# K and V loaded by even and odd partitions in a decode attention kernel

## The chip, the cores and the metric

The kernel runs on one core of one Trainium2 chip. The metric is device time in microseconds, measured on the chip; a lower time is better.

## The reference

Two branches share an input `x` of four tokens (batch 4, one query position, width 512) and are mixed by a gate of each token. The first is attention over the last 4096 positions of a long cache, with 32 query heads on 8 key heads; the second is a gated feed-forward layer. Cut to what matters:

```python
g = sigmoid((x * gate_w).sum(-1, keepdims=True))
# attention: B=4, Hq=32, Hkv=8, Dh=128, Sk=16384, window W=4096
q = (x @ wq).reshape(B, 1, Hq, Dh).transpose(0, 2, 1, 3)
k = repeat(k_cache[:, :, Sk - W:, :], 4, axis=1)
v = repeat(v_cache[:, :, Sk - W:, :], 4, axis=1)
p = softmax(einsum("bhqd,bhkd->bhqk", q, k) * Dh ** -0.5)
a = einsum("bhqk,bhkd->bhqd", p, v).transpose(0, 2, 1, 3).reshape(B, 1, Hq * Dh) @ wo
# feed-forward, F=1792
gate = x @ W_gate; up = x @ W_up
b = ((gate * (gate > 0)) * up) @ W_down
out = g * a + (1 - g) * b
```

All inputs are bfloat16. The window of K and of V is 32 MB each; with the weights 81 MB are read.

## The kernel before

The attention is worked in eight sets. A set is half of a batch entry: four of its eight key heads, 4096 keys each, so 4 MB of K and 4 MB of V. `Ksb` holds two sets of K (set `s` in half `s % 2`), `Vsb` one set of V; before that `Vsb` holds `wq`.

**Layout of a set.** The 4096 keys of a head are cut into 32 rows of 128 keys. Partition 4r + h of `Ksb` and `Vsb` holds row r of head h (`heads`, L245): 128 keys of 128 elements, 32 KB without a break. One transfer brings a set of K, and one a set of V.

**A set's work.** `turned` (L366) transposes K in blocks of 32 x 32 words on VectorE (DVE), in two halves of 4096 words a partition; a word is two bfloat16 elements. Its output `KT` has the elements on the partitions, and on the free side 2048 words a head: the word of head h, row r lands at 2048h + 8n + r%8, so that the 32 words of one block (4 heads, 8 rows) go to 32 places, the heads 2048 words apart. `scores` (L371) multiplies these by the queries `qS` into the PSUM tile `SB`. `highest` (L382) takes the maximum of each query head, with a small product on PE to turn it, and leaves `negmax`. `powers` (L392) forms the exponentials on ScalarE (ACT) and spreads them by four products into `PB`. `evicted` (L400) copies `PB` to `pP` in two halves on ACT, in the order of K's partitions, and adds them up. `turned_p` (L407) transposes `pP` on DVE, `values` (L414) multiplies with V on PE ("PV"), `summed` (L424) adds the parts, and `select` and `normal` (L434, L438) divide by the sum.

**Order of the work.** Each engine runs its own list of instructions in the order in which the program writes them. In a set DVE does the maximum, then the first half of the next set's K transpose, `normal` of the set before, the two transposes of P, the second half of the next K transpose, and `summed`. PE runs the eight sets as a loop (`emit`, L132); the other engines but SyncE run their lists inside `once` (L114), a loop body that is run one time. SyncE (SP) runs its list straight.

**Order of the loads.** All large loads are issued by SP, in this order: `wq`, K0, K1, V0, K2, V1, ... K7, V6, gate and up weights, V7, down weights, and `wo` in six parts into the place of `KT`. SP waits before an issue: K of set s for the K transpose of set s - 2 (`KTC`), V of set s for PV of set s - 1, `wo` for the last scores. A wait that names an instruction counted on a semaphore which PE reads is turned into a wait for the next instruction of that engine on the engine's own semaphore (`need`). The semaphore `V` is shared by `wq` and all V loads; PE lowers it by one set's count in each turn. At the end SP waits for both halves of the output row on `fin` and stores it.

Of the kernel before, what the change touches and what calls it, by code (L numbers as in the profile page):

```python
# [7 lines left out]
ACTF = mybir.ActivationFunctionType  # L8
# [4 lines left out]
SK = 16384  # L13
WIN = 4096
# [14 lines left out]
class Program:  # L29
# [101 lines left out]

    def emit(self, nc, engine, eng, sems):  # L132
        ops = self.ops[engine]
        if engine == "sp":
            self.emit_list(eng, sems, engine, ops, {}, {})
            return
        with self.once(nc, engine, eng):
            if engine != "pe":
                self.emit_list(eng, sems, engine, ops, {}, {})
                return  # L140
            t = self.turns
            self.emit_list(eng, sems, engine, ops[:t[0]], {}, {})
            first = self.signature(t[0], t[1], {})
            for k in range(1, len(t) - 1):
                shift = {s: k * n for s, n in self.lowered.items() if s not in self.shared}
                assert self.signature(t[k], t[k + 1], shift) == first, k
            turn = eng.alloc_register("pe_set")
            eng.reg_mov(turn, 0)
            eng.br("pe_loop")
            with nc.body("pe_loop", valid_engines=bass.OrderedEngineSet([eng.engine])):  # L150
                self.emit_list(eng, sems, engine, ops[t[0]:t[1]], {}, {}, turn)
                eng.drain()  # L152
                for s, n in self.lowered.items():
                    eng.sem_inc(sems[s], -n)
                eng.reg_add(turn, turn, 1)
                eng.br_lt(turn, len(t) - 1, on_true="pe_loop", on_false="pe_loop_end")
            nc.switch_bb("pe_loop_end")
            shift = {s: (len(t) - 1) * n for s, n in self.lowered.items() if s not in self.shared}
            self.emit_list(eng, sems, engine, ops[t[-1]:], shift, {})


def bass_gated_mix__sliding_block_cached__glu_gated_reglu__decode_kernel(
# [13 lines left out]
    with ExitStack() as ctx:  # L176
        def sb(name, shape, dt):
            return ctx.enter_context(nc.sbuf_tensor(name, shape, dt))

        def ps(name, width):  # L180
            return ctx.enter_context(nc.psum_tensor(name, [128, width], FP32))

        Ksb = sb("Ksb", [128, 2, 16384], BF16)
        Vsb = sb("Vsb", [128, 16384], BF16)
        KT = sb("KT", [128, 8192], FP32)
# [26 lines left out]
        p = sb("p", [128, 512], BF16)  # L212
        pP = sb("pP", [128, 2048], BF16)
# [9 lines left out]
        outr = sb("outr", [4, 512], BF16)  # L223
        SB = ps("SB", 512)
        PB = ps("PB", 2048)
# [3 lines left out]

        Kw = Ksb[:, :, :].rearrange("p s w -> p (s w)").bitcast(FP32).rearrange("p (s w) -> p s w", s=2)  # L230
        Kt = KT[:, :].bitcast(BF16).rearrange("p (h c v r o) -> p h c v r o", h=4, v=2, r=8, o=2)
        Kn = KT[:, :].rearrange("p (h n r) -> p n r h", h=4, r=8)
        qall = Wff[:, 0:4096]
        qrow = Wff[:, 4096:5120]
        hrelu = Kw[:, 0, 0:FQ]
# [6 lines left out]
        P = Program()  # L242
        P.events[("V", -1)] = ("V", 16, None, 0)

        def heads(cache, s):  # L245
            b, half = s // 2, s % 2
            return cache[b, 4 * half:4 * half + 4, SK - WIN:SK, :].rearrange("h (r c) d -> r h (c d)", r=32)

        def load_k(s):
            P.dma("sp", lambda e: e.dma_start(Ksb[:, s % 2, :], heads(A_k_cache, s)), ("K", s),  # L250
                  [("KTC", s - 2, 1)] if s >= 2 else [])

        def load_v(s):
            P.dma("sp", lambda e: e.dma_start(Vsb[:, :], heads(A_v_cache, s)), ("V", s),
                  [("PV", s - 1) if s else ("Q",)], sem="V")
            P.events[("V", s)] = ("V", 32, None, 0)

        P.op("dve", lambda e: e.memset(xs[:, :], 0.0), ("XS0",))
        for b in range(4):
            P.dma("act", lambda e, b=b: e.dma_start(xs[b:128:32, :], A_x[b].rearrange("o (a c) -> (o a) c", a=4)),  # L260
                  ("X", b), [("XS0",)])
        P.dma("act", lambda e: e.dma_start(xs[4:128:32, :], gate_w.rearrange("(a c) -> a c", a=4)), ("X", 4), [("XS0",)])
        load_k(0)
        for s in range(1, NSET):
            load_k(s)
            load_v(s - 1)
        P.dma("sp", lambda e: e.dma_start(Wff[:, 0:4 * FF], B_W_gate.rearrange("(p t) f -> p (t f)", p=128)), ("WG",), [("QT", 1)])
        P.dma("sp", lambda e: e.dma_start(Wff[:, 4 * FF:8 * FF], B_W_up.rearrange("(p t) f -> p (t f)", p=128)), ("WU",), [("QT", 1)])
        load_v(NSET - 1)
        P.dma("sp", lambda e: e.dma_start(Wd[:, :, :].rearrange("p i w -> p (i w)"),  # L270
                                          B_W_down.rearrange("(p i) w -> p (i w)", p=128)), ("WD",))
        wo_src = A_wo.rearrange("(p i) w -> p i w", p=128)
        for k in range(len(WO_CUTS) - 1):
            lo, hi = WO_CUTS[k], WO_CUTS[k + 1]
# [90 lines left out]

        def turned(s, u):  # L366
            lo = 4096 * u
            P.op("dve", lambda e: e.transpose(Kn[:, 128 * u:128 * u + 128], Kw[:, s % 2, lo:lo + 4096]), ("KTC", s, u),  # L368
                 [("K", s), ("SC", s - 1, u) if s else None], sem="vd")

        def scores(s):  # L371
# [28 lines left out]
        def evicted(s):  # L400
            for k in range(2):
                P.op("act", lambda e, k=k: e.activation(  # L402
                    pP[:, 1024 * k:1024 * k + 1024].rearrange("p (c r h) -> p c r h", r=8, h=4),
                    PB[:, :].rearrange("p (h c r) -> p c r h", h=4, r=8)[:, 32 * k:32 * k + 32], ACTF.Copy,
                    accum_out=rows[:, 2 * (s % 2) + k:2 * (s % 2) + k + 1]), ("PTE", s, k), [("PERM", s), ("RS", s - 2) if s > 1 else None])

        def turned_p(s):  # L407
# [49 lines left out]
        def units():  # L457
# [11 lines left out]
                ("H",), [("H2",), ("G",), ("HT0",)], sem="vd")  # L469

        turned(0, 0)
        turned_q(0)
        P.op("dve", lambda e: e.memset(osum[:, 0:64], 0.0), ("PTT", -1, 0), sem="vd")
        P.op("dve", lambda e: e.memset(mrow[:, 0:1], 0.0), ("PTT", -1, 1), sem="vd")
        turned(0, 1)
        turned_q(1)
        P.op("dve", lambda e: e.memset(osum[:, 64:129], 0.0), ("OSB", -1), sem="vd")
        for s in range(NSET):
            load_q(s)
            P.turn_edge()  # L480
            scores(s)
            highest(s)
            powers(s)
            evicted(s)
            select(s - 1)
            if s < NSET - 1:
                turned(s + 1, 0)
            else:
                P.op("dve", lambda e: e.memset(zz[:, :], 0.0), ("KTC", NSET, 0), sem="vd")
            if s:  # L490
                normal(s - 1)
            turned_p(s)
            P.op("pe", "aside")
            if s == NSET - 1:
                at = len(P.ops["pe"])
                gateup()
                P.aside = (at, len(P.ops["pe"]))
                units()
            else:
                turned(s + 1, 1)  # L500
            values(s)
            summed(s)
# [31 lines left out]
        for u in range(2):  # L534
# [3 lines left out]
        P.op("act", lambda e: e.copy(outr[:, 256:512], AB[32:36, 256:512]), ("FIN", 1), [("ACC", 1)], sem="fin")  # L538

        P.op("pool", None, None, [("ACC", 1)])  # L540

        per = {sem: P.events[b][1] - P.events[a][1] for sem, a, b in (
            ("vd", ("MX", 1), ("MX", 2)), ("va", ("EXP", 1), ("EXP", 2)), ("pq", ("QS", 1, 3), ("QS", 2, 3)))}
        per["V"] = 16
        P.shared["V"] = True
        P.lowered = per

        names = list(P.ENGINES) + ["vd", "va", "pq", "pro", "fin"] + P.dmas + ["done"]
        sems = {name: ctx.enter_context(nc.semaphore(name)) for name in names}
        nc.sync.dma_start(Vsb[:, :], A_wq.rearrange("(p t) w -> p (t w)", p=128)).then_inc(sems["V"], 16)  # L550
        with nc.Block() as block:
            @block.sync
            def _(e):
                P.emit(nc, "sp", e, sems)
                e.wait_ge(sems["fin"], 2)
                e.dma_start(out.rearrange("b o d -> (b o) d"), outr[:, :]).then_inc(sems["done"], 16)

            @block.gpsimd
            def _(e):
                P.emit(nc, "pool", e, sems)  # L560

            @block.tensor
            def _(e):
                P.emit(nc, "pe", e, sems)

            @block.vector
            def _(e):
                P.emit(nc, "dve", e, sems)

            @block.scalar  # L570
            def _(e):
                P.emit(nc, "act", e, sems)
# [29 lines left out]
```

## Time and profile before

| | us |
|---|---|
| median of three runs | 214.65 (213.74 to 215.91) |
| profiled execution | 215.62 |
| its span, first to last instruction | 214.1 |
| DVE busy | 167.4 (78%) |
| PE busy | 101.4 (47%) |
| ACT busy | 30.9 (14%) |

The transfers read 81.01 MB at a mean of 378 GB/s, and the mean granted clock of TensorE (PE) was 0.85. The span is the time between the first and the last instruction; the profiled execution's own time is a little longer than it. A share of busy time is a mean over the lead-in, the eight sets and the tail, which have different limits.

In the rows of the profile, L368 is line 368 of the kernel; "out<-in" names the tiles; "x16" is the number of instructions in a group, and the figures behind the bar are busy time in us, the mean duration in ns, and the idle time of the engine just before the group with what ended it. In the chain of waits a row is the start, the length and the work. SPq is SP's queue of issues.

### The profile page before, as it was taken

How to read it: one execution, taken by the hardware profiler on the slowest of the kernel's cores; microseconds unless marked ns; L12 is line 12 of the kernel's file. 1: busy time of each engine (PE TensorE's matmuls, PEld its weight loads, DVE VectorE, ACT ScalarE, POOL GpSimd, SP SyncE). 2: the span in 40 equal slices, each digit the busy share in tenths (PEclk: the TensorE clock that was granted, in tenths of full speed). 3: DMA queues.
4: the chain of work that ended last, by engine and by line, in shares of the span. 5: the costliest groups of instructions: out<-in, count | busy, mean ns of one | idle time of the engine just before them, and what ended most of it. 6: DMA issues, size and time to landing. Idle time of an engine off the chain costs nothing.

```text
span 214.1 us, 1792 instructions
## 1 busy us (share of the span) xinstructions
PE 101.4 (47%) x693; PEld 45.0 (21%) x701; DVE 167.4 (78%) x121; ACT 30.9 (14%) x49; POOL 15.4 (7%) x54
## 2 busy tenths in 40 slices
PE   0007433535650763085309430843195329477895
PEld 0002001112320331032104210320042013234362
DVE  0001799699989998999899989999998999745500
ACT  1100550040013003100400050005000500150000
POOL 7006110100010001000100100010001000000000
PEclk9999999999998599759966975796559656966999
DMA  7999999996399999998999799999977998898980
GB/s 288 398 454 429 398 484 392 380 410 288 98 404 478 392 386 398 453 429 318 465 410 465 300 465 416 392 386 398 441 343 294 392 433 351 331 453 384 415 328 4
DMA packets 4050, 81.03 MB, mean 378 GB/s; under 512 B 460, under 2 KB 976, under 8 KB 1232
## 3 DMA queue, kind: packets, MB, share of 16 engines
q1 hardware_dynamic: 4008, 81.01, 90.2%
q14 instruction: 2, 0.02, 0.0%
q10 hardware_dynamic: 40, 0.01, 0.0%
HBM read 81.01 MB, written 0.00 MB: 378 GB/s over the span
## 4 chain that ended last, share of the span: by engine, by line
DVE 65%; DMA 16%; PE 10%; issue 5%; PEldq 2%; PEld 1%; SPq 0%
DVE KT L368 47%; DMA Ksb<-in_A_k_cache_dram 10%; DVE pT L409 7%; DMA Vsb<-in_A_v_cache_dram 6%; PE AB L506 4%; DVE osum L431 3%; PE OB L419 3%; DVE mx L384 2%; PE FO L386 2%; PEldq L152 2%; DVE osb L425 1%; DVE on L442 1%; DVE oT L444 1%; DVE mrow L388 1%; PE SB L376 1%
## 5 line engine op out<-in xcount | busy, mean ns | idle before, releaser
L368 DVE STREAM_TRANSPOSE KT<-Ksb 128x4096 f32<-128x4096 f32 x16 | 116.5, 7282 | 4.8 <-DMA Ksb<-in_A_k_cache_dram 4.8
L419 PE MATMUL OB<-Vsb,pT 128*64 128x512 bf16 x256 | 44.8, 527 | 48.7 <-DVE pT L409 46.6
L419 PEld LDWEIGHTS OB<-Vsb,pT 128*64 128x64 bf16 x256 | 19.5, 150 | 73.2 <-DVE pT L409 51.7
L376 PE MATMUL SB<-KT,qS 128*32 128x512 bf16 x256 | 19.4, 428 | 19.9 <-DVE KT L368 8.4
L394 ACT ACTIVATE p<-SB,negmax 128x512 bf16<-128x512 f32 x8 | 5.5, 687 | 125.9 <-DVE negmax L388 125.9
L409 DVE STREAM_TRANSPOSE pT<-pP 128x1024 bf16<-128x1024 bf16 x16 | 18.8, 1211 | 0.2
L402 ACT ACTIVATE pP<-PB 128x1024 bf16<-128x1024 f32 x16 | 16.2, 1019 | 11.4 <-PE PB L397 11.4
L362 POOL COPY qS<-qT 32x64 bf16<-32x64 bf16 x32 | 7.3, 229 | 135.7 <-PE SB L376 125.3
L376 PEld LDWEIGHTS SB<-KT,qS 128*32 128x32 bf16 x256 | 9.2, 146 | 30.2 <-DVE KT L368 12.0
L397 PE MATMUL PB<-p,perm 128*128 128x512 bf16 x24 | 8.5, 476 | 11.1 <-ACT p L394 11.1
L315 DVE STREAM_TRANSPOSE xz<-xs 128x128 bf16<-128x128 bf16 x1 | 0.3, 312 | 15.7 <-DMA xs<-in_gate_w_dram 15.7
L322 PE MATMUL FO<-zr,onesf 128*128 128x4 f32 x2 | 0.6, 364 | 17.7 <-DVE zr L320 17.7
L431 DVE TENSOR_REDUCE osum<-osb 128x128 f32<-128x512 f32 x8 | 8.6, 1070 | 0.3
L425 DVE TENSOR_TENSOR osb<-OB,emask 128x512 f32<-128x512 f32 x8 | 5.4, 672 | 3.9 <-PE OB L419 3.9
L386 PE MATMUL FO<-identw,mx 128*128 128x128 f32 x16 | 4.2, 348 | 8.6 <-DVE mx L384 8.6
L506 PE MATMUL AB<-KT,oq 128*36 128x512 bf16 x30 | 6.6, 379 | 0.0
L537 DVE CAST outr<-AB 4x256 bf16<-4x256 f32 x1 | 0.4, 411 | 7.6 <-PE AB L509 7.6
L388 DVE CUSTOM_DVE_ANT_0 mrow<-FO,qmask 128x128 f32<-128x128 f32 x8 | 2.3, 292 | 4.9 <-PE FO L386 4.9
L384 DVE TENSOR_REDUCE mx<-SB 128x1 f32<-128x512 f32 x8 | 5.4, 679 | 0.9 <-PE SB L376 0.9
L397 PEld LDWEIGHTS PB<-p,perm 128*128 128x128 bf16 x32 | 2.8, 107 | 13.1 <-ACT p L394 10.5
L386 PEld LDWEIGHTS FO<-identw,mx 128*128 128x128 f32 x16 | 2.6, 202 | 12.8 <-DVE mx L384 12.8
L342 PE MATMUL PB<-Wff,rall 128*128 128x512 bf16 x8 | 3.8, 626 | 3.1 <-ACT Wff L346 2.0
(66 smaller groups left out, 64.8 us busy)
## 6 DMA issues: line engine op xcount, KB each, us to landing
Ksb<-in_A_k_cache_dram SPq DMA_DIRECT2D x8, 4096.0 KB, 18.7
Vsb<-in_A_v_cache_dram SPq DMA_DIRECT2D x8, 4096.0 KB, 12.4
Vsb<-in_A_wq_dram SPq DMA_DIRECT2D x1, 4096.0 KB, 12.3
Wff<-in_B_W_gate_dram SPq DMA_DIRECT2D x1, 1792.0 KB, 16.2
Wff<-in_B_W_up_dram SPq DMA_DIRECT2D x1, 1792.0 KB, 19.8
Wd<-in_B_W_down_dram SPq DMA_DIRECT2D x1, 1792.0 KB, 16.1
KT<-in_A_wo_dram SPq DMA_DIRECT2D x1, 1536.0 KB, 17.3
KT<-in_A_wo_dram SPq DMA_DIRECT2D x1, 1024.0 KB, 19.4
```

The costliest lines, as they stand in the source:

```text
L362: P.op("pool", lambda e, src=src, dst=dst: e.tensor_copy(dst, src[:, :, :, b, :]), ("QS", s, a), [("QT", half), ("QS", s, a - 1) if a else ...
L368: P.op("dve", lambda e: e.transpose(Kn[:, 128 * u:128 * u + 128], Kw[:, s % 2, lo:lo + 4096]), ("KTC", s, u), [("K", s), ("SC", s - 1, u) ...
L376: P.op("pe", lambda e, u=u, vo=vo, h=h: e.matmul(SB[32 * h:32 * h + 32, :], qS[:, 16 - 16 * u:48 - 16 * u, 4 * h + vo], Kt[:, h, 64 * u:64 ...
L384: P.op("dve", lambda e: e.tensor_reduce(mx[:, :], SB[:, :], AXIS.X, ALU.max), ("MX", s), [("SC", s, 1)], sem="vd")
L386: P.op("pe", lambda e: e.matmul(FO[:, 128:256], mx[:, 0:1].to_broadcast([128, 128]), identw[:, :], start=True, stop=True), ("MT", s), [("M ...
L397: P.op("pe", lambda e, h=h: e.matmul(PB[:, 512 * h:512 * h + 512], perm[:, h, :], p[:, :], start=True, stop=True), ("PERM", s) if h == 3 e ...
L402: P.op("act", lambda e, k=k: e.activation(pP[:, 1024 * k:1024 * k + 1024].rearrange("p (c r h) -> p c r h", r=8, h=4), PB[:, :].rearrange( ...
L409: P.op("dve", lambda e, k=k: e.transpose(pT[:, :].rearrange("p (u c q) -> p c u q", u=2, c=64)[:, 32 * k:32 * k + 32], pP[:, 1024 * k:1024 ...
L419: P.op("pe", lambda e, g=g, blk=blk, n=n: e.matmul(OB[64 * g:64 * g + 64, :], pT[:, 64 * blk:64 * blk + 64], Vsb[:, 512 * blk:512 * blk + ...
L425: P.op("dve", lambda e: e.tensor_tensor(osb[:, :, :], OB[:, :].rearrange("p (e d) -> p e d", e=4), emask[:, :].rearrange("p (e o) -> p e o ...
L431: P.op("dve", lambda e: e.tensor_reduce(osum[:, 0:128], osb[:, :, :].rearrange("p e d -> p d e"), AXIS.X, ALU.add), ("OSB", s), [("OM", s) ...
L506: P.op("pe", lambda e: e.matmul(AB[0:36, :], stat, mov, start=start, stop=False), None, waits)
```

## The change

K and V of a set are loaded by two transfers each, one to the even and one to the odd partitions. Partition 8a + 2h + b now holds row 2a + b of head h, so that two neighbouring rows of a head lie side by side. K's transpose then writes the 32 words of a block as 16 runs of two neighbouring words; `KT` itself holds the same words in the same places as before, and the products on it are the same. `evicted` puts P into the new order of partitions and reads `PB` in runs of two. The two transfers of a K share one semaphore, and those of a V count twice on theirs. K's load waits for `NEGMAX` of set s - 2 instead of its K transpose. SP's list runs inside `once` like those of the other engines, and the store of the output becomes the last entry of that list.

```diff
     def emit(self, nc, engine, eng, sems):
         ops = self.ops[engine]
-        if engine == "sp":
-            self.emit_list(eng, sems, engine, ops, {}, {})
-            return
         with self.once(nc, engine, eng):
...
-        Kn = KT[:, :].rearrange("p (h n r) -> p n r h", h=4, r=8)
+        Kn = KT[:, :].rearrange("p (h n b) -> p n h b", h=4, b=2)
...
-        def heads(cache, s):
+        def rows_of(cache, s, w):
             b, half = s // 2, s % 2
-            return cache[b, 4 * half:4 * half + 4, SK - WIN:SK, :].rearrange("h (r c) d -> r h (c d)", r=32)
+            return cache[b, 4 * half:4 * half + 4, SK - WIN:SK, :].rearrange("h (a b c) d -> b a h (c d)", a=16, b=2)[w]
 
         def load_k(s):
-            P.dma("sp", lambda e: e.dma_start(Ksb[:, s % 2, :], heads(A_k_cache, s)), ("K", s),
-                  [("KTC", s - 2, 1)] if s >= 2 else [])
+            for w in range(2):
+                P.dma("sp", lambda e, w=w: e.dma_start(Ksb[w:128:2, s % 2, :], rows_of(A_k_cache, s, w)), ("K", s, w),
+                      [("NEGMAX", s - 2)] if s >= 2 else [], sem="K%d" % s)
+            P.events[("K", s)] = ("K%d" % s, 32, None, 0)
 
         def load_v(s):
-            P.dma("sp", lambda e: e.dma_start(Vsb[:, :], heads(A_v_cache, s)), ("V", s),
-                  [("PV", s - 1) if s else ("Q",)], sem="V")
-            P.events[("V", s)] = ("V", 32, None, 0)
+            for w in range(2):
+                P.dma("sp", lambda e, w=w: e.dma_start(Vsb[w:128:2, :], rows_of(A_v_cache, s, w)), ("V", s, w),
+                      [("PV", s - 1) if s else ("Q",)], sem="V")
+            P.events[("V", s)] = ("V", 48, None, 0)
...
         def turned(s, u):
             lo = 4096 * u
-            P.op("dve", lambda e: e.transpose(Kn[:, 128 * u:128 * u + 128], Kw[:, s % 2, lo:lo + 4096]), ("KTC", s, u),
+            P.op("dve", lambda e: e.transpose(Kn[:, 512 * u:512 * u + 512], Kw[:, s % 2, lo:lo + 4096]), ("KTC", s, u),
...
                 P.op("act", lambda e, k=k: e.activation(
-                    pP[:, 1024 * k:1024 * k + 1024].rearrange("p (c r h) -> p c r h", r=8, h=4),
-                    PB[:, :].rearrange("p (h c r) -> p c r h", h=4, r=8)[:, 32 * k:32 * k + 32], ACTF.Copy,
+                    pP[:, 1024 * k:1024 * k + 1024].rearrange("p (n h b) -> p n h b", h=4, b=2),
+                    PB[:, :].rearrange("p (h n b) -> p n h b", h=4, b=2)[:, 128 * k:128 * k + 128], ACTF.Copy,
...
+        P.dma("sp", lambda e: e.dma_start(out.rearrange("b o d -> (b o) d"), outr[:, :]), ("OUT",), [("FIN", 1)], sem="done")
...
-        per["V"] = 16
+        per["V"] = 32
...
                 P.emit(nc, "sp", e, sems)
-                e.wait_ge(sems["fin"], 2)
-                e.dma_start(out.rearrange("b o d -> (b o) d"), outr[:, :]).then_inc(sems["done"], 16)
```

More of the change, by code (lines that the diff above doesn't have):

```diff
@@ L540, in bass_gated_mix__sliding_block_cached__glu_gated_reglu__decode_kernel @@
         P.op("pool", None, None, [("ACC", 1)])
+        P.dma("sp", lambda e: e.dma_start(out.rearrange("b o d -> (b o) d"), outr[:, :]), ("OUT",), [("FIN", 1)], sem="done")
         per = {sem: P.events[b][1] - P.events[a][1] for sem, a, b in (
             ("vd", ("MX", 1), ("MX", 2)), ("va", ("EXP", 1), ("EXP", 2)), ("pq", ("QS", 1, 3), ("QS", 2, 3)))}
-        per["V"] = 16
+        per["V"] = 32
         P.shared["V"] = True
         P.lowered = per
-        names = list(P.ENGINES) + ["vd", "va", "pq", "pro", "fin"] + P.dmas + ["done"]
+        names = list(P.ENGINES) + ["vd", "va", "pq", "pro", "fin"] + P.dmas
         sems = {name: ctx.enter_context(nc.semaphore(name)) for name in names}
```

## The prediction, made before the changed kernel was run

> **What bounds the kernel now.** I read the page first, for the share of each engine and of the transfers, then the chain of waits, then the transfers in stretches, then single rows.
>
> ```profile
> span 214.1 us, 1792 instructions
> DVE  0001799699989998999899989999998999745500
> DMA  7999999996399999998999799999977998898980
> q1 hardware_dynamic: 4008, 81.01, 90.2%
> ```
>
> Two resources stand close together. VectorE (DVE) is nearly solid from the fifth slice to the thirty-fifth, and the 16 DMA engines are busy for 90.2% of the span with 81.01 MB. Which of them sets the pace shows in the chain, here one of the eight sets (a set is half a batch: four heads):
>
> ```profile
> 121.58 1.07 DVE osum L431
> ...
> 124.13 0.01 DVE negmax L388
> 124.14 7.12 DVE KT L368
> 131.26 0.04 DVE rc L441
> ...
> 132.17 2.37 DVE pT L409 x2
> 134.55 7.33 DVE KT L368
> 141.87 0.52 DVE osb L425
> ...
> 142.48 1.08 DVE osum L431
> 143.56 0.61 DVE mx L384
> ```
>
> From one L431 to the next it is 142.48 - 121.58 = 20.9 us, DVE row after DVE row, with waits only for the small products around the maximum. Two transposes of K make 14.5 us of it on the chain (2 x 7.28 = 14.6 by instruction), and everything else 6.3 us. So the middle is bound by DVE.
>
> The transfers follow it closely:
>
> ```profile
> 5.00:40.00 35.00, 1.00 1.00 431
> 41.00:44.00 3.00, 1.00 0.83 284
> 53.80:57.40 3.60, 1.00 0.00 0
> 57.40:160.60 103.20, 0.79 0.97 406
> 160.60:162.20 1.60, 1.00 0.00 0
> ```
> ```profile
> Ksb<-in_A_k_cache_dram SPq DMA_DIRECT2D x8, 4096.0 KB, 18.7
> Vsb<-in_A_wq_dram SPq DMA_DIRECT2D x1, 4096.0 KB, 12.3
> Wff<-in_B_W_gate_dram SPq DMA_DIRECT2D x1, 1792.0 KB, 16.2
> ```
>
> The stretch columns are window, length, granted TensorE clock, DMA share, GB/s. With a full queue the rate is 431 GB/s, so 4096 KB (4.194 MB) take 9.73 us and 1792 KB 4.26 us. One set needs K and V, 19.46 us of transfer, against 20.9 us of DVE. The transfers have only 1.4 us of slack in a set: whatever DVE gains beyond that is not seen in the period.
>
> **The change part by part.**
>
> *K's transpose, L368.* Same words in, same count; the words of a 32-word run now go out as 16 pairs of neighbours instead of 32 words that each lie 2048 words from the one before.
>
> ```profile
> L368 DVE STREAM_TRANSPOSE KT<-Ksb 128x4096 f32<-128x4096 f32 x16 | 116.5, 7282 | 4.8 <-DMA Ksb<-in_A_k_cache_dram 4.8
> L444 DVE STREAM_TRANSPOSE oT<-on 32x128 f32<-32x128 f32 x8 | 3.2, 395 | 0.3
> L351 DVE STREAM_TRANSPOSE qT<-Wff 128x1024 f32<-128x1024 f32 x2 | 2.4, 1200 | 0.0
> L464 DVE STREAM_TRANSPOSE Ksb<-Ksb 128x448 f32<-128x448 f32 x1 | 0.6, 645 | 0.0
> ```
>
> L351 and L464 write neighbouring words: (1200 - 645)/(1024 - 448) = 0.96 ns a word and 213 ns fixed. L444 writes words four apart and comes to (395 - 213)/128 = 1.42 ns; L368 to (7282 - 213)/4096 = 1.73 ns. So a scattered word costs up to 0.76 ns extra. No row writes pairs. Lower end: a pair hides the extra, 213 + 4096 x 0.96 = 4.2 us (4.8 if L351 is simply scaled by four). Middle: the extra is paid once per pair, 5.7 us. Upper end: nothing changes, 7.3 us. A pair is nearer to L351 than to single words; I take 4.9 us. The choice matters little: DVE's set becomes 2 x 4.9 + 6.3 = 16.1 us, and DVE falls below the transfers' 19.46 us for any price under 6.6 us.
>
> [...]
>
> *The loop through PE.* With DVE out of the way the loop is: PV products, scores of the next set, its maximum, K's transpose, `normal`, P's transpose, PV again.
>
> ```profile
> 133.47 5.02 PE L419 MATMUL OB<-Vsb,pT 128*64 128x512 bf16 x32 [7.13 <-DVE pT L409]
> 154.38 6.50 PE L419 MATMUL OB<-Vsb,pT 128*64 128x512 bf16 x32 [6.82 <-DVE pT L409]
> 162.04 2.06 PE L376 MATMUL SB<-KT,qS 128*32 128x512 bf16 x32 [1.16 <-PEq L154]
> ```
>
> PV 5.0 to 6.5 us, the loop's turn and both halves of the scores 1.16 + 2.06 = 3.2, maximum to K's next transpose 1.5 (in the chain 121.58 + 1.07 = 122.65 to 124.14), transpose 4.9, `normal` 0.9 (131.26 to 132.17), first half of P's transpose 1.2: 16.8 to 18.3 us. That too is under 19.46, by at least 1.2 us.
>
> *The wait of K's load.* It moves from the K transpose two sets back (which SP sees at the next counted DVE instruction, L428) to `NEGMAX`.
>
> ```profile
> 80.02 0.07 DVE osum L428
> ...
> 82.64 0.01 DVE negmax L388
> ```
> ```profile
> 56.10 0.54 SPq L254 DMA_DIRECT2D Vsb<-in_A_v_cache_dram  x1
> ...
> 80.05 0.54 SPq L250 DMA_DIRECT2D Ksb<-in_A_k_cache_dram  x1
> ```
>
> That is 2.6 us later. Behind it on SP waits only the next V, whose own release (PV done) comes some 14 us later, so V is not held. In the new order K's issue falls about 10.5 us after a V has landed (PV 5.5, scores 3.2, maximum 1.5), while the next V keeps the queue full until about 19.5 us: cost nothing. V's issue is the tighter one: PV ends up to 6.5 us after V has landed, landing trails the last bytes by about half a microsecond, and first bytes follow an issue by 57.4 - 56.10 = 1.3 us. Together 8.3 us, under the 9.73 us of the K load in flight: 1.4 us to spare.
>
> *Two loads for one.* 16 more issues on SP at 0.54 us, four instead of two in a set; SP otherwise waits, and the second half is issued while the first flows. Same bytes, same 32 KB rows, same set of 128 partitions in the end. What a load on every other partition yields, no row shows. Bounds: the full 431 GB/s, 9.73 us for two halves, or half of it, 19.46 us, as if only half of the memory's inputs could be used at once; a gain is excluded since the queue was full at 431. The nearest row is the whole load with the same rows and bytes; I take 9.73.
>
> *The rest.* ACT's L402 reads pairs from PSUM instead of single words; even twice its 1 us a half would end before P's transpose, which stands behind K's on DVE. SP inside `once` adds a few register instructions, hidden by `A_wq` in flight for 12.3 us. The output's issue and its waits keep their place.
>
> *The sum*, if the queue stays full from the start until the last V:
>
> ```profile
> 1.27 21.47 DMA Ksb<-in_A_k_cache_dram
> ...
> 181.58 12.40 DMA Vsb<-in_A_v_cache_dram
> ...
> 211.51 0.39 DVE outr L537
> ```
>
> K of set 0 lands at 22.74. Then come 15 loads of 9.73 (7 K, 8 V) = 146.0 and two of 4.26 = 8.5 (gate and up, ahead of the last V): the last V lands at 177.2 instead of 193.98. From there to the span's end it was 214.1 - 193.98 = 20.1 us, PV, down and output products, whose own loads follow V in the queue as before: 197.3. The 16.7 us come from the empty stretches (3.6 + 1.6), the slow one at 284 GB/s, and 406 GB/s instead of 431 over 103 us. The profiled execution took 215.62, 1.5 more than its span, and lay 1.0 above the median of 214.65; so 197.3 + 1.5 - 1.0 = **198 us**.
>
> Own range 195 to 204: down if the tail tightens, up by a slow stretch of 3 us and a price of 5.7 us with PV at 6.5.
>
> **The rivals.**
>
> *Slower: the half loads don't reach the rate.* The source of a half load has 16 slices of 2 rows x 128 keys (`a`), four heads each. If each of 16 DMA engines takes one slice, then it writes partitions 8a, 8a+2, 8a+4, 8a+6, and all engines in step sit at the same place in their eights: half of the neighbourhoods of four partitions are written by two engines each, half by none. For it: no load in the trace is of this kind. Against it: the same 32 KB rows run at 431 now, and engines out of step would not meet. Price: 13.0 (K of set 0 lands at 22.74, 9.73 before that `A_wq`) + 16 L + 8.5 + 20.1 + 0.5, with L the time of one K or V (9.73 gives the 198 again). It decides from L = 10.8 us on (389 GB/s), where the result is 214.65. Two cases: engines that meet half of the time, L = 14.6, **276 us**, with anything from 214 to 300; and always, 19.46, 353 us.
>
> [...]
>
> *Gaps in the queue.* The 1.4 us before V's issue is lost to a slow PE clock, and each of seven sets pays up to 1.3 us of first-byte latency: 203 to 211 us, say 207. For it: PV already took 6.5 us; against it: 5.0 to 5.5 is usual.
>
> *The transposes stay at 7.3 us,* the change not doing what it says: DVE's 20.9 us a set stays, K's later issue is covered, 215 us. L444 speaks against it.
>
> **How the numbers follow.** Forecast 0.41; half loads that meet in part 0.27, always 0.19; gaps 0.08; unchanged transposes 0.05. The half loads together weigh a little more than the forecast, since nothing in the trace bears on them either way, but over 140 us; 198 is the likeliest case. A measurement of this kernel (213.74 to 215.91) can tell about 1% from no change. Faster by over 1%: 0.41 + 0.06 = 0.47. Within 1%: 0.02 of the gaps, 0.04 of the transposes, 0.01 of the half loads = 0.07. Slower: 0.26 + 0.19 + 0.01 = 0.46. The range reaches from 195 through the case at 276 to 300 and leaves out the 0.19 of the case at 353.
>
> **What would show it.** Right: L368 near 4.9 us, L431 to L431 about 19.5 us, DVE idle before PV or before K with DMA as releaser, DMA at 9 in nearly every slice, 431 GB/s in mid-run. Wrong: GB/s well under 400 with the queue full (half loads), zeros in the stretches (gaps), L368 above 6.6 us.

## The result, and the profile after

The changed kernel takes 357.72 us (355.59 to 359.72) against 215.28 us before, a ratio of 1.67 (95% interval 1.65 to 1.68). A few executions of a kernel run some 2% longer than its others; medians and ranges here hold them all, ratios leave the longer ones out. The forecast of 198 us was wrong; the time is that of the second case of the rival "half loads" (353 us), which the range of 195 to 300 us left out.

The page of the changed kernel, the same parts as shown of before:

```profile
span 354.3 us, 1812 instructions
DVE  0012919121660329020850349030931267036030
DMA  8999989999999899899999998998999989898993
GB/s 333 319 192 222 233 185 233 218 196 237 207 207 233 185 233 233 185 233 207 207 237 196 218 233 185 233 226 189 237 196 218 233 189 229 295 345 189 267 413 122
q1 hardware_dynamic: 4264, 81.01, 98.1%
```

DVE has long empty stretches. The DMA engines are busy for 98.1% of the span, more than before, with the same 81.01 MB: they are not idle, they are slow, at 185 to 237 GB/s in the slices in which only K and V come in. The rate returns only with the weights at the end, 295, 345 and 413 GB/s in three of the last six slices. The groups and the issues:

```profile
L368 DVE STREAM_TRANSPOSE KT<-Ksb 128x4096 f32<-128x4096 f32 x16 | 70.8, 4426 | 70.6 <-DMA Ksb<-in_A_k_cache_dram 70.6
L419 PE MATMUL OB<-Vsb,pT 128*64 128x512 bf16 x256 | 44.5, 523 | 192.8 <-DMA Vsb<-in_A_v_cache_dram 192.8
```
```profile
Ksb<-in_A_k_cache_dram SPq DMA_DIRECT2D x16, 2048.0 KB, 39.4
Vsb<-in_A_v_cache_dram SPq DMA_DIRECT2D x16, 2048.0 KB, 28.1
```

The transpose did get cheaper, from 7.28 to 4.43 us, and DVE now waits 70.6 us for K and PE 192.8 us for V. The chain of waits, one set:

```profile
117.06 0.54 SPq L254
117.60 0.04 issue
117.64 32.40 DMA Vsb<-in_A_v_cache_dram
150.04 0.14 issue
150.17 5.18 PE OB L419 x32
155.35 0.02 issue
155.37 0.54 SPq L254
155.91 0.04 issue
155.95 33.12 DMA Vsb<-in_A_v_cache_dram
```

From one V issue to the next it is 155.37 - 117.06 = 38.3 us, and the chain holds nothing but loads of V (each queued behind a K) and PV. The mean rate over 250 us in the middle (window, length, clock, DMA share, GB/s):

```profile
40.00:290.00 250.00, 0.67 1.00 214
```

At 214 GB/s the 4.194 MB of a K or V take 19.6 us, twice the 9.73 of before. The single packets of the trace, each a row of 32 KB, say the same: of the 1635 that start in these 250 us every one took 2.3 to 2.6 us, where the median before is 1.21. So the engines did not stand idle between rows (a share of 1.00); each row took twice as long.

### The profile page after: what moved, and what is told of

The parts are those of the page before. It is cut to its first block, busy times and chain, and to the rows that moved or that the text cites. A ratio compares the mean times of both kernels' runs of the same rounds, so it can differ in the third digit from the quotient of the medians.

```text
span 354.3 us, 1812 instructions
## 1 busy us (share of the span) xinstructions
PE 99.7 (28%) x693; PEld 48.3 (14%) x701; DVE 125.1 (35%) x121; ACT 30.8 (9%) x49; POOL 15.4 (4%) x54
## 3 DMA queue, kind: packets, MB, share of 16 engines
q1 hardware_dynamic: 4264, 81.01, 98.1%
HBM read 81.01 MB, written 0.00 MB: 229 GB/s over the span
## 4 chain that ended last, share of the span: by engine, by line
DMA 79%; PE 15%; SPq 1%; issue 1%; ACTq 1%; PEldq 1%; DVE 1%; PEld 0%; DVEq 0%
DMA Vsb<-in_A_v_cache_dram 74%; PE OB L419 11%; DMA xs<-in_gate_w_dram 5%; PE AB L506 3%; SPq L254 1%; PE PB L335 1%; ACTq L260 1%; PEldq L149 1%; PEld OB L419 0%; PE FO L322 0%; DVE on L442 0%; DVE oT L444 0%; DVE outr L537 0%; PE AB L509 0%; PE FO L435 0%
## 5 line engine op out<-in xcount | busy, mean ns | idle before, releaser
L419 PE MATMUL OB<-Vsb,pT 128*64 128x512 bf16 x256 | 44.5, 523 | 192.8 <-DMA Vsb<-in_A_v_cache_dram 192.8
L368 DVE STREAM_TRANSPOSE KT<-Ksb 128x4096 f32<-128x4096 f32 x16 | 70.8, 4426 | 70.6 <-DMA Ksb<-in_A_k_cache_dram 70.6
L419 PEld LDWEIGHTS OB<-Vsb,pT 128*64 128x64 bf16 x256 | 21.6, 149 | 215.1 <-issue 211.5
L376 PE MATMUL SB<-KT,qS 128*32 128x512 bf16 x256 | 18.3, 425 | 16.1 <-PEq L151 7.6
L376 PEld LDWEIGHTS SB<-KT,qS 128*32 128x32 bf16 x256 | 10.7, 143 | 23.7 <-issue 10.6
L506 PEld LDWEIGHTS AB<-KT,oq 128*36 128x36 bf16 x30 | 4.2, 139 | 2.3
L435 PE MATMUL FO<-osum,S 128*16 128x129 f32 x18 | 4.4, 337 | 0.0
```

Of the source, the lines that this page charges most:

```text
L368: P.op("dve", lambda e: e.transpose(Kn[:, 512 * u:512 * u + 512], Kw[:, s % 2, lo:lo + 4096]), ("KTC", s, u), [("K", s), ("SC", s - 1, u) ...
L376: P.op("pe", lambda e, u=u, vo=vo, h=h: e.matmul(SB[32 * h:32 * h + 32, :], qS[:, 16 - 16 * u:48 - 16 * u, 4 * h + vo], Kt[:, h, 64 * u:64 ...
L419: P.op("pe", lambda e, g=g, blk=blk, n=n: e.matmul(OB[64 * g:64 * g + 64, :], pT[:, 64 * blk:64 * blk + 64], Vsb[:, 512 * blk:512 * blk + ...
L506: P.op("pe", lambda e: e.matmul(AB[0:36, :], stat, mov, start=start, stop=False), None, waits)
```

## The experiments

Three theories of the slow loads, guesses of the author, were set against each other. "Slices": the source's slowest dimension is shared out over the 16 DMA engines, here one slice each, and in step two engines write into one group of partitions and slow each other. Which engine takes which slice is not in the trace; how slices are shared out and what makes a group are assumptions of this theory, in the expectations below too. "Halves": a load on every other partition is slow as such. "Pitch": memory is slow when the engines read 64 KB apart.

### The split alone, with 32 slices

```diff
-  cache[b, 4*half : 4*half+4, ...].rearrange("h (r c) d -> r h (c d)", r=32)      # Ksb[:, s % 2, :]
+  cache[b, 4*half+w : 4*half+4 : 2, ...].rearrange("h (r c) d -> r h (c d)", r=32) # Ksb[w:128:2, s % 2, :], w = 0, 1
```

> The kernel before with one edit: each K and V comes in two loads, on the even and on the odd partitions, as in the change, but with the partitions of before (4r + h), so that a half load has 32 slices of two heads where the change has 16 slices of four. Theory 'slices' (with 16 slices each of the 16 DMA engines gets one slice, that is a run of eight neighbouring partitions, and in step two engines write into one group of four partitions while half of the groups stand idle; with 32 slices an engine gets two slices half a quadrant pattern apart and the groups are shared out evenly): a 32 KB row stays at 1.21 us, a set of K and V at 19.5 us of transfer, time within 1% of before, 213 to 218 us. Theory 'halves' (a load on every other partition is slow as such, whatever its slices): rows near 2.44 us, 345 to 360 us. Theory 'pitch' (memory is slow when the engines read 64 KB apart; here rows are 32 KB apart): as before, 213 to 218 us.

Measured: 214.8 us, ratio 0.999 (0.993 to 1.005). A stretch with the queue full, 24 to 40 us:

```profile
24.00:40.00 16.00, 1.00 0.99 428
```

Two loads on the even and odd partitions, at the full 428 GB/s. "Halves" is out, and so are 16 more issues on SP as a cause.

### The change's loads alone

```diff
+  for w in range(2): dma(Ksb[w:128:2, s % 2, :], rows_of(A_k_cache, s, w))   # V the same; all else as before
```

> The kernel before with the change's loads alone (even and odd partitions, 16 slices of four heads); K's transpose, the wait of K's load, SP's list and the copy of P stay as before, so that the rows of keys stand in another order than the transposes take them for. All three theories of the loads (slices, halves, pitch): 350 to 360 us, the transposes back at 7.28 us hidden behind the loads. If the later wait of K's load, SP's list or the copy of P had a part in the loss, it is lower by that part: below 345 us.

Measured: 359.86 us. The same stretch:

```profile
24.00:40.00 16.00, 0.64 1.06 223
```

The loads alone make the whole loss; the later wait of K, SP's list and the copy of P have no part in it that this run, a single one, could show.

### Whole loads with 16 slices

```diff
-  cache[b, 4*half : 4*half+4, SK-WIN : SK, :].rearrange("h (r c) d -> r h (c d)", r=32)
+  cache[b, 0:8, SK - 2048*(2-half) : SK - 2048*(1-half), :].rearrange("h (a c) d -> a h (c d)", a=16)
```

> The kernel before with one edit: a set's K and V come in one load each over all 128 partitions, but with a source of 16 slices of eight heads (half of the keys of twice the heads, so the data are others than the set's; same bytes, same 32 KB rows, slices 32 KB apart in memory). Theory slices: each engine writes eight neighbouring partitions, four in one group and four in the next, in step with a second engine: rows 2.44 us, L = 19.5 us a load, 345 to 360 us. Theory halves: all partitions in one load, so rows 1.21 us and 213 to 218 us. Theory pitch: 32 KB apart as before, 213 to 218 us.

Measured: 365.69 us.

```profile
24.00:40.00 16.00, 1.00 1.08 223
```

One load over all 128 partitions, slices 32 KB apart, and still half the rate. Neither the halves nor the pitch can do that; 16 slices can.

### The pitch alone

```diff
-  cache[..., SK-WIN : SK, :].rearrange("h (r c) d -> r h (c d)", r=32)
+  cache[..., SK-2*WIN : SK, :].rearrange("h (r o c) d -> o r h (c d)", r=32, o=2)[0]
```

> The kernel before with one edit: the load of a set takes every second row of 128 keys from twice the window (other keys than the reference's; same bytes and rows), so that the 32 slices lie 64 KB apart in memory as in the change, on the partitions of before. Theory pitch: rows near 2.44 us, 345 to 360 us. Theories slices and halves: rows 1.21 us, 213 to 218 us.

Measured: 215.55 us.

```profile
24.00:40.00 16.00, 0.51 0.99 428
```

"Pitch" is out.

### Only K in halves

```diff
-  V: two loads with rows_of(...)
+  V: one load with heads(...), 32 slices, as before      # K as in the change
```

> The changed kernel with V loaded whole as before and K alone in halves (K and V rows in different orders). If each half-loaded tile costs 19.5 us and each whole one 9.73, with the queue full: first K lands at 13.0 + 19.5 = 32.5, then 7 x (19.5 + 9.7) + 9.7 + 8.5 = 222.6, then the tail of 20.1: a span of 275 us, 274 to 280 us. If the slow rate came from something that the split turns on for all loads, 340 us or more.

Measured: 281.99 us, 2 us above the range, a span of 279.6 against 275 expected. Stretches inside a K load (32 to 50 and 91 to 109) and inside a V load:

```profile
32.00:50.00 18.00, 0.50 1.00 213
52.00:60.00 8.00, 0.50 0.92 397
91.00:109.00 18.00, 0.78 1.08 231
111.00:119.00 8.00, 0.50 0.95 406
```

The slow rate belongs to each load by itself and switches from one to the next on the same queue.

### Four engines or two on a group

Sixteen slices may be slow wherever they land, or because of where they land. Two runs load V by eight loads of 16 rows, by the theory one row for each engine: on 16 neighbouring partitions, and on 16 partitions eight apart. Both read the same rows of memory in the same order.

```diff
+  for g in range(8): dma(Vsb[16*g : 16*g+16, :], rows16(A_v_cache, s, g))   # neighbours
+  for g in range(8): dma(Vsb[g : 128 : 8, :], rows16(A_v_cache, s, g))      # eight apart
```

> The kernel before with V's load alone changed: eight loads of 16 rows of one head, each on 16 neighbouring partitions (rows in another order than the products take them for; same bytes, same 32 KB rows, 16 slices, one row for each engine). Four engines then write into each group of four partitions at a time. Theory groups (one group of four partitions takes what one engine brings): rows 4.85 us, 38.8 us for V, first K at 22.7, then 7 x 9.7 + 8 x 38.8 + 8.5, and the tail of 20.1: a span near 430 us. Theory sixteen slices (a load that gives each engine one slice runs at half rate, wherever it lands): rows 2.44 us, a span near 275 us.

> [...] Theory groups: rows 2.44 us, 19.5 us for V, 22.7 + 7 x 9.7 + 8 x 19.5 + 8.5 + 20.1: a span near 275 us, 155 us below the run with neighbours. Theory sixteen slices: the same time as with neighbours. [...]

Measured: neighbours 397.81 us (span 396.6), eight apart 284.09 us (span 282.1). The stretches, a V load and a K load of each, first with neighbours, then eight apart:

```profile
77.00:104.00 27.00, 0.55 0.95 118
108.00:118.00 10.00, 0.53 0.94 360
```
```profile
62.00:80.00 18.00, 0.56 1.00 208
82.00:90.00 8.00, 0.61 0.92 397
```

The place decides: with the same slices and rows, 118 GB/s on neighbours and 208 eight apart, against 431 with the loads of before. Sixteen partitions eight apart lie in sixteen different fours of neighbours. If only rows on one and the same four slowed each other, a row would have taken 1.21 us as before, with a time near 215 us. By the stretch from 62 to 80 us it took 16 x 32768 bytes x 1.00 / 208 GB/s = 2.52 us, twice that. The 2.44 us of the second expectation counts two rows to a group here too; that was an assumption of the author, and which partitions make up a group no run shows. The change's loads, at 214 GB/s, fit the same picture if the engines work in step, one slice each: they then write partitions eight apart.

"Groups" comes near both times (spans near 430 and 275 us expected, 396.6 and 282.1 measured), with one size off: neighbours came out 33 us faster than expected, some 4.2 us a V. The stretch shows why: from 77 to 104 us a row of V took 16 x 32768 bytes x 0.95 / 118 GB/s = 4.22 us, not four times 1.21 = 4.85. If four rows share a group, as the theory has it, a group took 4 x 32768 bytes in 4.22 us, 31 GB/s by this estimate, where a row of before came at 27 (32768 bytes in 1.21 us). No run has 16 slices at the full rate; that 16 slices are slow only by their place rests on these two runs.

### The change without its split loads

```diff
-  for w in range(2): dma(Ksb[w:128:2, s % 2, :], rows_of(A_k_cache, s, w))
+  dma(Ksb[:, s % 2, :], heads(A_k_cache, s))               # V the same; all else as in the change
```

> The changed kernel with its split loads alone undone: one load each over all 128 partitions from the source of before (so the rows of keys stand in another order than the transposes and the copy of P take them for); runs of two words, the copy in pairs, the later wait of K's load and SP's list stay. If the loads were the whole loss and the prediction's other terms hold: transposes 4.4 us, 196 to 202 us, below the kernel before by 6 to 8%. If the later wait or SP's list costs something: above the run with pairs of heads by that.

Measured: 206.13 us (204.11, 204.28, 207.97 and 208.24) against 215.52 before on the same chip. With whole loads the rest of the change is worth 9 us by the median and 11 by the two lowest times, not the 17 forecast.

### Runs of two words without touching the loads

Pairs can also be made of two heads of one row, which already lie on neighbouring partitions; then only the layout of `KT` changes.

```diff
-  Kt = ....rearrange("p (h c v r o) -> p h c v r o", h=4, v=2, r=8, o=2)
-  Kn = ....rearrange("p (h n r) -> p n r h", h=4, r=8)
+  Kt = ....rearrange("p (g c v r k o) -> p g k c v r o", g=2, v=2, r=8, k=2, o=2)
+  Kn = ....rearrange("p (g n k) -> p n g k", g=2, k=2)
```

> The kernel before, its loads untouched, with KT laid out so that two heads of one row stand side by side (two groups of two heads): K's transpose writes runs of two words, and the scores read KT every 8 bytes instead of every 4. If the sum of the prediction was right but for the loads: K's transpose 4.4 us as in the changed kernel, the queue of loads full, a set 19.5 us, 196 to 202 us. If a full queue of loads or the loop through PE holds it back instead: 203 to 212 us. If the scores read slower at 8 bytes, their products get longer than 0.43 us each, and up to 2 us a set come on top.

Measured: 205.64 us, ratio 0.962 (0.951 to 0.972): faster than both kernels, but above the 196 to 202 expected. Its groups:

```profile
L368 DVE STREAM_TRANSPOSE KT<-Ksb 128x4096 f32<-128x4096 f32 x16 | 70.8, 4424 | 5.1 <-DMA Ksb<-in_A_k_cache_dram 5.1
L376 PE MATMUL SB<-KT,qS 128*32 128x512 bf16 x256 | 32.4, 660 | 10.9 <-PEq L154 7.8
```

The transpose is 4.42 us. The score products take 660 ns each, where the group of the kernel before has 428:

```profile
L376 PE MATMUL SB<-KT,qS 128*32 128x512 bf16 x256 | 19.4, 428 | 19.9 <-DVE KT L368 8.4
```

Longer products are not what holds it: the run before, with products as short as ever (424 ns), takes the same time. The chain goes through V:

```profile
108.94 13.56 DMA Vsb<-in_A_v_cache_dram
128.97 14.81 DMA Vsb<-in_A_v_cache_dram
149.85 13.33 DMA Vsb<-in_A_v_cache_dram
```

A set takes (149.85 - 108.94)/2 = 20.5 us, not 19.5. The stretches before and after V is asked for:

```profile
104.00:110.00 6.00, 0.70 1.00 431
110.00:114.00 4.00, 1.00 0.99 377
...
150.00:153.00 3.00, 1.00 0.59 208
```

V is issued at 108.94 and at 149.85, and just behind that the rate falls: the K load in flight is through before V's first bytes come. (After the issue at 68.03 it does not fall; the margin is thin and not lost in every set.)

### Four heads side by side

```diff
+  Kt = ....rearrange("p (c v r h o) -> p h c v r o", h=4, v=2, r=8, o=2)
+  Kn = KT, 32 words without a break
```

> As the run with pairs of heads, but with all four heads of a row side by side: K's transpose writes its 32 words without a break, and the scores read KT every 16 bytes. Transpose 4.2 to 4.5 us (pairs already hide the extra). If the scores read at 16 bytes as fast as before: the same time as with pairs, 196 to 202 us. If a read every 16 bytes costs PE what a write every 16 bytes costs DVE (1.7 of a word's time), scores 2.1 become 3.5 us a set, hidden as long as the loads set the pace: 196 to 204 us.

Measured: 221.21 us, ratio 1.029 (1.021 to 1.038), slower than before and not what was expected.

```profile
L368 DVE STREAM_TRANSPOSE KT<-Ksb 128x4096 f32<-128x4096 f32 x16 | 70.8, 4422 | 4.8 <-DMA Ksb<-in_A_k_cache_dram 4.8
L376 PE MATMUL SB<-KT,qS 128*32 128x512 bf16 x256 | 61.0, 1103 | 9.6 <-PEq L154 7.7
```

A longer run gains DVE nothing over pairs (4.42 us both), but the products read `KT` every 16 bytes now and take 1103 ns. That is 61.0/8 = 7.6 us a set where 19.4/8 = 2.4 was, and the loop through PE becomes the bound: these products are the largest part of the chain of waits (27.9%), and the loads run at 374 GB/s between 60 and 140 us.

### V asked for in two halves

If the loads hold the pairs back, it is because V is asked for late. Here V comes in two halves of its columns over all partitions, the first released half way through PV.

```diff
-  dma(Vsb[:, :], heads(A_v_cache, s), after PV of s - 1)          # PV's products reordered, to read the first half first
+  for k in range(2): dma(Vsb[:, 8192*k : 8192*k+8192], heads(A_v_cache, s)[:, :, 8192*k : 8192*k+8192],
+                         after PV product 15 (k = 0) or 31 (k = 1) of s - 1)
```

> The run with pairs of heads (K's transpose in runs of two, whole loads over all partitions), and V loaded in two halves of its columns over all 128 partitions, the first half issued as soon as the first sixteen PV products are done (their order follows the columns). In the run with pairs a set took 20.4 us instead of 19.5 and V was issued only when the K load in flight was nearly through. If that late issue is what the queue lost: V's first half is asked for some 3 us earlier, a set goes to 19.5 to 19.8 us, the gap before the last V (1.7 us) closes, 198 to 202 us. If the queue was full and the loads themselves run at 10.1 us a tile: no change against 205.6 us (203 to 208 us).

Measured: 197.39 us (197.23 to 197.57), ratio 0.915 (0.908 to 0.922), the fastest of all and a little below the range. The stretch from 60 to 140 us in the run with pairs, and in this one:

```profile
60.00:140.00 80.00, 0.83 0.99 418
```
```profile
60.00:140.00 80.00, 0.80 1.00 430
```

With V released earlier the queue runs at 430 GB/s, and a set is 2 x 4.194 / 0.430 = 19.5 us. The rows of these V loads are 16 KB instead of 32; whether that helps by itself, no run shows.

## Why the prediction was wrong, point by point

*What bounds the kernel before: right.* Taking DVE's load away without hurting the transfers brought 206 us and then 197 us.

*The transpose: right in kind, a little high.* 4.43 us measured, 4.9 taken, near the lower end of 4.2. Pairs of heads cost 4.42 us, a full run of 32 words 4.42 as well: with pairs, what a longer run could gain is already gained.

*Two loads for one: the step that failed.* The prediction bounded a K or V by 9.73 and 19.46 us and took the lower end, because the whole load was "the nearest row". It was nearest in bytes and rows, but not in what decided here: the slices, 16 at 214 GB/s where 32 ran at 428. The value was the other end, 19.6 us at 214 GB/s, and 16 loads of it make the whole difference. The rival's own sum, 13.0 + 16 x 19.46 + 8.5 + 20.1 = 353.0, meets the span of 354.3. The argument put against it, that engines out of step would not meet, did not hold: of 1635 rows in 250 us not one ran at the old 1.21 us. The rival's own picture was wrong in one point: in step, 16 engines on 32 fours of neighbours stand one on a four, not two. That rows slow each other even so, the run with partitions eight apart shows (208 GB/s); that two engines on one neighbourhood of four do so was an assumption of the rival, and what makes them meet no run shows. So the price of 353 us came out right by the bound of half the rate, which in this is luck: the mechanism as given would not have brought it. The halves of the partitions had no part in it: with 32 slices they cost nothing (ratio 0.999). The chance of 0.19 for the full loss was too low, and the range that left it out was too narrow.

*The later wait and SP's list: right,* as far as the runs can tell: with them 206.13 us, without them, in the run with pairs of heads, 205.64; these two differ in the length of the products as well.

*The sum with full loads: right only with a step more.* "1.4 us to spare" before V's issue was too optimistic. The term that was mis-sized is the time that the K load in flight lasts beyond V's landing: 9.73 us less half a microsecond by the prediction (0.37 us before, from 193.61, the end of the last row of the last V, to its landing at 193.98). In the run with pairs V lands at 102.92 and the rate falls from 110, some 7 us later, while V's first bytes are due 6.0 + 1.3 = 7.3 us after the landing. So with whole loads the sets took 20.5 us and the time was 206, the case called "gaps in the queue" (203 to 211). With V released in halves the span is 196.2, where the sum gave 197.3. The prediction's list of where its 16.7 us come from adds up to 12.2; it leaves out, above all, ten microseconds at 334 GB/s (44 to 54 us), 2.3 us more. The sum does not use the list.

## What to carry to other kernels

When a load's shape changes, count the slices of its slowest dimension and look at which partitions they fill: 16 slices ran at 214 GB/s where 32 ran at 428, with the same bytes, the same length of row and the same even and odd partitions, and loads of 16 rows ran at 118 on neighbouring partitions and at 208 on partitions eight apart. If no row of the trace has the new shape, similar bytes are no reason to take the good end of the bounds. And a cheaper layout for the writer may be had inside the destination, without touching the transfer, as long as the reader's stride stays small: read every 8 bytes it paid here (ratio 0.962), every 16 it did not (1.029).

## What the hardware showed beyond that

Score products on PE got slower with the stride at which they read `KT`: 428 ns at 4 bytes, 660 ns at 8, 1103 ns at 16. DVE's transpose went the other way and only once: 7.28 us with single scattered words, 4.42 with pairs, 4.42 without a break.
